# A new instruction order for a delta-rule attention and MLP kernel, with the clock-filler matmuls in other places

## Chip, core and metric

The kernel runs on one core of a Trainium2 chip. The metric is device time in microseconds for one execution of the whole program, all loads and stores included; lower is better.

## What is computed

Four batches of eight heads run a delta rule over 768 steps with head dimension 48. The result, reshaped to (4, 768, 384), goes through a layer norm without bias and a two-layer MLP with a residual. The reference, cut to its core:

```python
k_n = k / (norm(k, axis=-1) + 1e-6)
for t in range(S):                                   # S = 768
    y[:, :, t] = einsum('bhd,bhde->bhe', q[:, :, t], state)
    v_old = einsum('bhde,bhd->bhe', state, k_n[:, :, t])
    state = state + beta[:, :, t] * einsum('bhd,bhe->bhde', k_n[:, :, t], v[:, :, t] - v_old)
x = y.transpose(0, 2, 1, 3).reshape(4, 768, 384)
xn = (x - mean(x)) / sqrt(var(x) + 1e-6) * g_ln
out = x + maximum(xn @ w_ch1, 0) @ w_ch2             # 384 -> 1536 -> 384
```

The two weight matrices arrive as 64-bit floats; everything else is 32-bit.

## The kernel before

The sequence is cut into 12 chunks of 64 steps, and all 32 heads of a chunk are worked on at once.

**Per chunk, attention.** Keys and queries are loaded and turned (TensorE transposes, L555, or a DVE transpose, L577). The gram product of the keys is made in tiles of 48 rows by 32 columns (L606, later L674). From it comes the inverse of a small triangular matrix per head, by forward substitution on DVE: a long chain of short multiply and subtract instructions (L752/L759 for the first chunk, L843/L850 for pairs of later chunks). The query product (L637) is masked on DVE (L653). For chunk 0 only, two products (L806, with a copy on ACT, L809, between them) join the halves of the inverse, and DVE writes the result back (L813). Three small products (L902) with ACT copies (L908) and one DVE subtraction (L906) between them give the new values `u`; then come the output (L913), the state update (L923), and the reads of the state (L880).

**Per chunk, layer norm and MLP.** ACT copies the output out (L950). DVE and ACT make the statistics (L956 to L965) and the normalised rows (L968). They are transposed (L1000 on TensorE for the first three chunks, through DRAM later) and scaled into `xnt` (L1006, L1016). Chunks 0 to 2 use plain first-layer matmuls (L1178, 128x128 by 256 columns, six matmul records to a step); later chunks use a form with 15 products in place of 18 (L1094). The second layer is L1200 for chunk 0 and a form with seven products in place of eight (L1275) after it. These four lines use the whole 128x128 array.

**Weights.** Twelve pieces of 768 KB are loaded by ACT's DMA queue (L373), called p0 to p11 here. p0 to p5 are `w_ch1` (p0 to p2 hold the first half of its columns), p6 to p11 are `w_ch2`. Each is converted from 64 to 32 bits by two ACT instructions (L514, L522), one on DVE (L519) and one on GpSimd (L532). A staging buffer is free for its next piece when GpSimd has read it.

**Fillers.** Three steps of two 512-column matmuls on zeros (`fill`, L544) and 26 steps of two 256-column matmuls (`warm`, L1358) compute nothing that is used. They exist to keep TensorE's clock up while the first chunks are prepared. Once their constants exist, they wait for nothing but their place in TensorE's order.

**What sets the order.** The program builds a list of 2780 steps, and a tuple of step numbers, `ORDER`, says in which order they are emitted. Within one engine the emitted order is kept: each engine works through its own steps first in, first out, and an ACT or SyncE instruction that starts a load holds up those behind it until the load may start.

```python
    def emit(self, order):
        done = set()
        for n in order:
            s = self.steps[n]
            ...
            s.fn()
...
    def zeros():
        nc.tensor.matmul(f_[0][:, 256:512], ident, ident[:, 0:1].to_broadcast([128, 256]))
...
    with in_this_order(tc):
        line.emit(ORDER)
```

Of the kernel before, what the change touches and what calls it, by code (L numbers as in the profile page):

```python
# [57 lines left out]
def pool(n):  # L58
# [7 lines left out]
    18, 21, 5, 0, 6, 7, 78, 68, 20, 23, 9, 22, 24, 28, 125, 77, 70, 15, 8, 10, 12, 13, 30, 40, 27, 34, 31, 59, 16, 26, 29, 50, 33, 89, 39, 32, 35, 88,  # L66
    90, 60, 91, 92, 93, 25, 94, 126, 127, 61, 71, 1, 65, 47, 37, 38, 99, 128, 19, 129, 130, 131, 132, 133, 169, 135, 219, 2, 134, 136, 73, 100, 101,
    103, 102, 104, 36, 323, 137, 53, 321, 42, 138, 139, 140, 46, 63, 87, 76, 84, 56, 109, 107, 48, 322, 43, 352, 114, 105, 202, 115, 116, 106, 108,
    117, 118, 119, 120, 45, 51, 11, 74, 170, 324, 52, 58, 141, 142, 143, 4, 144, 145, 85, 146, 147, 148, 149, 150, 171, 151, 152, 44, 41, 96, 95, 121,
    98, 172, 153, 154, 155, 156, 157, 158, 159, 160, 161, 162, 163, 164, 165, 166, 167, 168, 174, 221, 124, 123, 57, 122, 3, 222, 55, 192, 97, 220,  # L70
    223, 173, 224, 17, 204, 225, 226, 228, 227, 230, 231, 232, 233, 234, 235, 236, 237, 238, 239, 240, 241, 175, 72, 83, 176, 177, 207, 14, 242, 243,
    208, 244, 245, 110, 111, 203, 54, 178, 246, 209, 113, 112, 179, 180, 200, 181, 86, 326, 293, 213, 206, 325, 182, 190, 194, 294, 211, 205, 183,
    247, 248, 229, 383, 249, 250, 251, 79, 252, 191, 703, 210, 328, 198, 217, 295, 296, 81, 297, 69, 298, 300, 362, 188, 253, 254, 255, 256, 257, 193,
    302, 299, 327, 301, 75, 258, 259, 357, 260, 305, 195, 199, 261, 215, 329, 336, 382, 303, 304, 306, 355, 310, 262, 263, 319, 311, 186, 307, 64,
    264, 265, 266, 267, 212, 268, 363, 333, 320, 269, 308, 184, 196, 330, 334, 842, 339, 82, 337, 840, 388, 341, 343, 387, 340, 66, 338, 342, 569,
    270, 312, 309, 317, 271, 272, 273, 187, 62, 313, 390, 201, 274, 389, 391, 49, 67, 189, 318, 275, 80, 185, 197, 392, 315, 214, 344, 331, 335, 316,
    314, 394, 276, 277, 278, 365, 353, 427, 367, 332, 358, 428, 425, 431, 393, 345, 279, 280, 426, 429, 281, 282, 283, 284, 285, 286, 287, 288, 289,
    290, 216, 350, 346, 432, 435, 218, 385, 564, 570, 430, 433, 349, 364, 291, 436, 354, 568, 292, 384, 705, 386, 395, 488, 439, 563, 368, 567, 566,
    565, 571, 434, 396, 707, 560, 715, 739, 561, 735, 437, 713, 487, 356, 366, 370, 489, 397, 360, 351, 398, 438, 464, 441, 399, 490, 491, 400, 440,
    492, 493, 359, 443, 401, 442, 404, 361, 372, 405, 407, 408, 411, 402, 562, 895, 494, 369, 495, 445, 371, 377, 406, 446, 465, 466, 449, 409, 403,  # L80
    450, 451, 452, 467, 497, 498, 410, 499, 500, 501, 502, 414, 415, 412, 503, 504, 505, 468, 572, 416, 506, 507, 413, 508, 573, 509, 444, 447, 373,
    453, 510, 374, 511, 574, 417, 512, 421, 704, 576, 454, 716, 513, 514, 422, 714, 515, 712, 717, 706, 701, 702, 734, 710, 708, 711, 718, 742, 746,
    748, 738, 743, 749, 375, 577, 376, 420, 423, 578, 419, 380, 424, 455, 448, 456, 516, 479, 378, 579, 418, 517, 518, 519, 580, 480, 469, 470, 457,
    458, 471, 520, 379, 381, 575, 581, 582, 521, 583, 709, 522, 841, 843, 839, 744, 1174, 733, 736, 747, 737, 745, 459, 606, 607, 523, 524, 525, 526,
    527, 528, 529, 530, 531, 460, 584, 461, 472, 473, 474, 475, 585, 719, 608, 612, 476, 724, 586, 587, 720, 481, 610, 532, 533, 482, 750, 723, 590,
    725, 613, 609, 614, 611, 616, 617, 615, 618, 721, 620, 722, 726, 619, 624, 534, 535, 536, 537, 588, 625, 589, 592, 591, 595, 538, 496, 485, 622,
    539, 483, 540, 541, 542, 543, 544, 545, 546, 547, 548, 549, 550, 484, 596, 597, 732, 621, 727, 728, 623, 639, 850, 640, 641, 642, 643, 626, 644,
    848, 628, 846, 851, 740, 993, 1209, 852, 1208, 478, 849, 730, 741, 729, 627, 731, 751, 752, 629, 847, 462, 838, 463, 994, 845, 1179, 630, 631,
    593, 594, 853, 1001, 1007, 477, 1004, 598, 551, 755, 602, 632, 633, 637, 636, 647, 646, 666, 667, 668, 669, 649, 650, 651, 1366, 645, 753, 756,
    893, 634, 890, 635, 638, 648, 600, 757, 605, 754, 656, 758, 759, 760, 604, 764, 761, 670, 763, 599, 601, 671, 657, 658, 652, 552, 553, 554, 555,  # L90
    556, 486, 557, 558, 672, 681, 762, 1173, 1172, 1207, 1000, 1005, 1175, 1003, 682, 683, 684, 653, 654, 685, 766, 655, 559, 854, 663, 659, 686, 674,
    660, 675, 676, 677, 678, 661, 1206, 1370, 1002, 997, 1006, 855, 856, 662, 891, 603, 767, 768, 769, 770, 771, 898, 899, 844, 999, 896, 858, 859,
    860, 857, 765, 772, 773, 775, 861, 892, 1008, 679, 687, 904, 900, 901, 680, 776, 862, 777, 778, 779, 863, 692, 693, 780, 781, 782, 783, 784, 1182,
    1177, 1187, 1181, 1367, 1185, 995, 998, 785, 906, 786, 689, 922, 664, 694, 695, 905, 925, 688, 864, 347, 787, 923, 788, 865, 789, 790, 791, 910,
    866, 1472, 1369, 1178, 1176, 1470, 792, 867, 793, 1183, 794, 1471, 795, 1009, 796, 1188, 869, 1364, 665, 673, 868, 870, 696, 697, 698, 902, 907,
    797, 911, 700, 872, 699, 1010, 916, 1184, 1363, 873, 798, 1186, 799, 1011, 917, 996, 800, 348, 903, 801, 877, 1205, 1012, 924, 1013, 897, 690,
    931, 871, 878, 1180, 874, 932, 933, 926, 934, 935, 875, 802, 1014, 803, 804, 912, 1015, 879, 805, 876, 806, 908, 807, 881, 808, 1016, 880, 909,
    913, 809, 882, 914, 928, 1017, 927, 810, 938, 918, 811, 915, 929, 1189, 936, 894, 919, 1018, 812, 884, 920, 939, 1019, 1628, 813, 885, 814, 958,
    886, 921, 959, 815, 937, 960, 930, 816, 1368, 961, 1022, 691, 940, 817, 1377, 1020, 818, 883, 819, 962, 1374, 820, 963, 821, 1204, 948, 822, 949,
    774, 1473, 823, 941, 964, 950, 824, 1469, 965, 951, 1021, 888, 952, 887, 1375, 955, 973, 825, 974, 1379, 1054, 953, 826, 1373, 942, 957, 827, 943,  # L100
    1631, 944, 1058, 1190, 954, 956, 1023, 1025, 945, 1210, 1194, 975, 976, 1026, 1191, 946, 1195, 1062, 1196, 947, 889, 828, 1029, 829, 1061, 1192,
    977, 830, 966, 1193, 1055, 1063, 967, 831, 968, 1056, 832, 978, 1059, 969, 833, 1057, 979, 970, 971, 1197, 972, 1030, 834, 1031, 1065, 835, 836,
    1202, 837, 1198, 1024, 1068, 1066, 1067, 1045, 984, 1069, 985, 1035, 986, 1199, 1203, 1027, 1070, 1047, 1200, 1028, 1201, 1032, 1212, 1071, 1060,
    1048, 1211, 987, 1064, 1213, 1072, 1049, 1033, 1034, 1074, 1052, 1036, 988, 989, 1073, 1037, 1081, 1376, 990, 1053, 1075, 1214, 1365, 1468, 1079,
    1050, 1215, 1632, 1076, 981, 1046, 1040, 1216, 1077, 1038, 1083, 1080, 1078, 1039, 1082, 1395, 1092, 1378, 1217, 1051, 1041, 1086, 1084, 1372,
    1095, 980, 1087, 1371, 1089, 1088, 1098, 1093, 1090, 1218, 1094, 1085, 1099, 1101, 1110, 1104, 1219, 1096, 1111, 1112, 1380, 1100, 1113, 1042,
    1114, 1105, 1115, 1091, 1102, 1120, 1641, 1116, 1220, 1103, 1044, 1636, 1107, 1097, 991, 1121, 1043, 1221, 1249, 983, 1222, 1108, 1925, 1246,
    1381, 1627, 1247, 1118, 1821, 1122, 1385, 1637, 1245, 1127, 1825, 1250, 1128, 1386, 1123, 1474, 1382, 1819, 1124, 1383, 1387, 1253, 982, 1384,
    992, 1117, 1125, 1388, 1823, 1106, 1630, 1109, 1129, 1393, 1119, 1126, 1137, 1389, 1390, 1138, 1139, 1248, 1391, 1140, 1252, 1396, 1141, 1251,
    1130, 1131, 1132, 1397, 1145, 1398, 1392, 1136, 1142, 1146, 1399, 1135, 1147, 1143, 1148, 1133, 1400, 1149, 1144, 1401, 1150, 1134, 1152, 1151,  # L110
    1153, 1403, 1224, 1402, 1154, 1163, 1254, 1256, 1223, 1404, 1227, 1255, 1394, 1155, 1405, 1225, 1258, 1156, 1406, 1164, 1228, 1407, 1232, 1157,
# [1362 lines left out]
```

## Time and profile before

| | |
|---|---|
| median of 3 runs | 510.86 us (510.31 to 513.01) |
| the profiled execution's own time | 511.47 us |
| its span, first to last instruction | 509.8 us |
| mean granted TensorE clock | 0.973 |
| busy | PE 96%, DVE 75%, POOL 48%, ACT 36% |
| matmuls | 9688 |

The profiled execution ran 0.61 us over the median, and 1.7 us of its time lies outside the span. In timeline rows the first number is the start in us from the span's start, the second the duration; what stands in square brackets is the engine's idle time before the row and what ended it. PEclk is the clock that was granted to TensorE as a share of full speed.

### The profile page before, as it was taken

How to read it: one execution, taken by the hardware profiler on the slowest of the kernel's cores; microseconds unless marked ns; L12 is line 12 of the kernel's file. 1: busy time of each engine (PE TensorE's matmuls, PEld its weight loads, DVE VectorE, ACT ScalarE, POOL GpSimd, SP SyncE). 2: the span in 40 equal slices, each digit the busy share in tenths (PEclk: the TensorE clock that was granted, in tenths of full speed). 3: DMA queues.
4: the chain of work that ended last, by engine and by line, in shares of the span. 5: the costliest groups of instructions: out<-in, count | busy, mean ns of one | idle time of the engine just before them, and what ended most of it. 6: DMA issues, size and time to landing. Idle time of an engine off the chain costs nothing.

```text
span 509.8 us, 21948 instructions
## 1 busy us (share of the span) xinstructions
PE 490.7 (96%) x9688; PEld 442.9 (87%) x9688; DVE 384.3 (75%) x854; ACT 185.4 (36%) x402; POOL 246.0 (48%) x377
## 2 busy tenths in 40 slices
PE   8669899999999999999999999999999999999996
PEld 5647787668898899999999989999999999999996
DVE  1886886989879997739999848999979889454241
ACT  3464864413532225162223434313431421424130
POOL 5122347111663267784191374391682581735544
PEclk9875899999999999999999999999999999999999
DMA  9984676454534550440363441530420302003011
GB/s 132 188 277 83 161 138 131 95 81 69 89 51 70 105 111 14 102 76 7 88 110 67 100 68 44 102 62 1 108 55 32 87 3 81 17 16 80 1 39 32
DMA packets 155855, 40.47 MB, mean 79 GB/s; under 512 B 149232, under 2 KB 152304, under 8 KB 155760
## 3 DMA queue, kind: packets, MB, share of 16 engines
q1 hardware_dynamic: 151760, 29.21, 31.8%
q10 hardware_dynamic: 3712, 9.83, 5.9%
q8 instruction: 76, 1.25, 1.0%
q14 instruction: 19, 0.16, 0.1%
q0 software_dynamic: 288, 0.03, 0.1%
HBM read 30.79 MB, written 8.26 MB: 77 GB/s over the span
## 4 chain that ended last, share of the span: by engine, by line
PE 89%; ACT 3%; DVE 2%; DMA 2%; issue 2%; SPq 1%; POOL 1%; ACTq 0%; DVEq 0%; POOLq 0%
PE f L1275 29%; PE f L1094 23%; PE f L1178 10%; PE two L902 6%; PE f L1200 3%; PE two L674 3%; PE by L913 2%; PE by L880 2%; PE two L880 2%; PE f L1358 2%; PE two L923 1%; DMA words<-in_moe_w_ch_dram 1%; PE two L637 1%; SPq L373 1%; ACT goff L627 1%
## 5 line engine op out<-in xcount | busy, mean ns | idle before, releaser
L1261 POOL TENSOR_TENSOR h_all<-h_all 128x256 f32<-128x256 f32 x99 | 75.5, 775 | 21.2 <-ACT h_all L1187 15.0
L1275 PE MATMUL f<-w_sb,h_all 128*128 128x192 f32 x396 | 81.6, 331 | 0.5 <-POOL xb L829 0.5
L850 DVE TENSOR_TENSOR xb<-xb,tmp 128x31 f32<-128x31 f32 (+15 forms) x186 | 75.8, 408 | 4.0
L1275 PE MATMUL f<-words,h_all 128*128 128x192 f32 x396 | 78.1, 331 | 0.7 <-DVE o L1293 0.7
L843 DVE TENSOR_TENSOR tmp<-xb,gb 128x31 f32<-128x31 f32 (+15 forms) x186 | 73.0, 392 | 4.3
L1107 DVE TENSOR_TENSOR h_all<-f,h_all 128x512 f32<-128x512 f32 x90 | 60.3, 683 | 20.0 <-PE f L1094 16.4
L1300 POOL TENSOR_TENSOR words<-h_all 128x128 f32<-128x128 f32 x66 | 30.3, 480 | 79.3 <-ACT h_all L1110 55.1
L1275 PEld LDWEIGHTS f<-words,h_all 128*128 128x128 f32 x396 | 65.1, 190 | 2.5 <-DVE o L1293 0.8
L1275 PEld LDWEIGHTS f<-w_sb,h_all 128*128 128x128 f32 x396 | 64.8, 190 | 2.2 <-POOL xb L829 0.8
L1178 PE MATMUL f<-xnt,w_sb 128*128 128x256 f32 x216 | 51.4, 386 | 0.5 <-DVE o L1293 0.5
L1102 ACT COPY h_all<-f 128x512 f32<-128x512 f32 x36 | 21.1, 586 | 72.7 <-PE f L1094 45.5
L1094 PE MATMUL f<-kt,w_sb 128*128 128x128 f32 x360 | 46.4, 277 | 0.0
L1110 ACT ACTIVATE h_all<-h_all 128x512 f32<-128x512 f32 x54 | 32.1, 625 | 38.5 <-DVE h_all L1107 38.4
L1178 PEld LDWEIGHTS f<-xnt,w_sb 128*128 128x128 f32 x216 | 39.7, 190 | 7.1 <-DVE o L1293 0.8
L1094 PEld LDWEIGHTS f<-kt,w_sb 128*128 128x128 f32 x360 | 43.4, 192 | 0.8 <-issue 0.4
L1094 PE MATMUL f<-xnt,w_sb 128*128 128x128 f32 x288 | 34.3, 276 | 0.0
L908 ACT COPY u<-two 128x768 f32<-128x768 f32 x24 | 19.1, 795 | 41.1 <-PE two L902 41.0
L1094 PEld LDWEIGHTS f<-xnt,w_sb 128*128 128x128 f32 x288 | 33.1, 192 | 0.1
L1293 DVE TENSOR_TENSOR o<-f,x 128x192 f32<-128x192 f32 x33 | 11.4, 348 | 22.7 <-PE f L1275 13.7
L1275 PE MATMUL f<-w_sb,words 128*128 128x192 f32 x132 | 28.2, 329 | 0.0
L532 POOL TENSOR_TENSOR w_sb<-words 128x768 uint32<-128x768 uint32 (+1 forms) x9 | 13.0, 1450 | 27.5 <-DVE words L519 15.2
L1293 POOL TENSOR_TENSOR o<-o,words 128x192 f32<-128x192 f32 x22 | 13.2, 608 | 26.9 <-DVE words L1293 23.4
(198 smaller groups left out, 883.2 us busy)
## 6 DMA issues: line engine op xcount, KB each, us to landing
words<-in_moe_w_ch_dram ACTq DMA_DIRECT2D x8, 768.0 KB, 5.7
v<-in_v_dram SPq DMA_DIRECT2D x24, 192.0 KB, 4.1
kr<-in_k_dram SPq DMA_DIRECT2D x46, 96.0 KB, 3.3
out_dram<-o SPq DMA_DIRECT2D x46, 96.0 KB, 2.4
xld<-xlt SPq DMA_DIRECT2D x9, 384.0 KB, 2.3
xnt<-xld SPq DMA_DIRECT2D x36, 96.0 KB, 2.8
tb<-in_q_dram SPq DMA_DIRECT2D x40, 64.0 KB, 2.6
tb<-in_k_dram SPq DMA_DIRECT2D x32, 64.0 KB, 3.2
```

The source lines that it names most:

```text
L843: lambda j=j, n=n, w=w, t=t: nc.vector.tensor_tensor(out=t, in0=xb[:, 0:n, j : j + 1].to_broadcast([128, n, w]), in1=gb[:, j : j + 1, j + ...
L850: "DVE", dve(n * w), lambda t=t, rest=rest: nc.vector.tensor_tensor(out=rest, in0=rest, in1=t, op=ALU.subtract),
L902: nc.tensor.matmul(*args(e, e ^ hp, 2 * j + hp))
L1094: nc.tensor.matmul(wide(p[:, 128 * n : 128 * n + 128]), w[:, 128 * n : 128 * n + 128], r, start=start and n == 0, stop=True, skip_group_ch ...
L1102: add("ACT", act(512), lambda: nc.scalar.copy(to[0], ps(p)), pk, to[1])
L1107: add("DVE", dve(512), lambda: nc.vector.tensor_tensor(out=to[0], in0=in0, in1=in1, op=op), [*pk, *y[1]], to[1])
L1110: add("ACT", act(512), lambda: nc.scalar.activation(to[0], to[0], ACTF.Relu), [], to[1])
L1178: nc.tensor.matmul(p[:, 0:TOK], w1_sb[:, t, f * 128 : (f + 1) * 128], xnt[:, t], start=(t == 0), stop=(t == KC - 1))
L1261: add(eng, cost, lambda: e.tensor_tensor(out=out_, in0=x, in1=y, op=op), r, w, port=2 if eng == "Pool" else 1)
L1275: lambda f=f, t=start and f == 0: nc.tensor.matmul(p[:, 0:D2], lhs(f), rhs[:, f], start=t, stop=(f == F2 - 1), skip_group_check=True),
L1293: lambda: e.tensor_tensor(out=out_, in0=a, in1=b_, op=ALU.add), r, w,
L1300: lambda f=f + i: e.tensor_tensor(out=s3[f], in0=one(0, 0)[0](f), in1=one(1, 0)[0](f), op=ALU.subtract),
```

## The change

Only `ORDER` differs: the same 2780 numbers in another sequence. The new sequence was made by a scheduler that takes the granted clock from the columns that matmuls stream, times the share of the array that they use, where the old one took it from the time that TensorE is busy. No step is added, removed or altered. Its first lines:

```diff
 ORDER = (
-    18, 21, 5, 0, 6, 7, 78, 68, 20, 23, 9, 22, 24, 28, 125, 77, 70, 15, 8, 10, 12, 13, 30, 40, 27, 34, 31, 59, 16, 26, 29, 50, 33, 89, 39, 32, 35, 88,
...
+    6, 7, 23, 5, 0, 59, 40, 60, 15, 8, 21, 4, 10, 20, 27, 16, 17, 219, 31, 26, 22, 69, 75, 29, 46, 35, 88, 89, 90, 67, 28, 25, 76, 92, 91, 93, 12, 94,
...
```

What that means for TensorE up to the first L1178 step (W = one `warm` step, F = one `fill` step; T0 to T3 = transposes of the keys of chunks 0 to 3, Tq0 and Tq1 of the queries, an a or b marks half of such a step pair; G = L606, Q = L637, J1 and J2 = the two L806 products, U1 to U3 = the three L902 products, Y = L913, S = L923, X = L1000, R = the first L880):

```
before: 4W F T0 F G0 F 2W T1a W T1b G1 4W T2 G2 2W J1 2W J2 Tq0 Q0 W T3a U1 T3b W U2 W U3 W
        Y W G3 S 2W Tq1 W X W X Q1 2W R L1178
after:  2F 2W T0 2W G0 3W F 3W T1 W G1 7W Tq0 T2 3W G2 Q0a W Q0b J1 J2 W U1 U2 T3a U3 W
        Y W T3b S W Tq1 X X G3 Q1 L1178
```

From U1 on there are ten W before the first L1178 step in the old order and three in the new one (one more W stands right ahead of U1 in the new order, and one ahead of T3a in the old one). The weight pieces are loaded in another sequence too:

```
before: p2 p6 p4 p3 p1 p0 p5 p8 p7 p9 p10 p11
after:  p2 p4 p0 p7 p6 p5 p1 p3 p9 p10 p8 p11
```

ACT's order around chunk 0's chain changes with it. In the new order a conversion of p0 (L522) stands directly ahead of the copy between J1 and J2 (L809), a conversion of p6 directly ahead of the copy after U1 (L908), and conversions of p4, p5 and p1 ahead of the copy after U3. On DVE two conversions of p2 (L519) move ahead of the transposes that make J1's operand (L774, L801), the mask of Q0 (L653) moves ahead of the first L843, and L813 follows 13 of the L843/L850 instructions where it followed 16. After the first L1178 step the same matmuls follow in a similar interleaving to the end. The very last GpSimd instructions change places: the sum that the last output needs (L1293) goes behind two others.

214 rows, old and new, of the table ORDER are left out of this document.

## The prediction

> **What bounds the kernel now.** I first read the page's totals and its slices.
>
> ```profile
> PE 490.7 (96%) x9688; PEld 442.9 (87%) x9688; DVE 384.3 (75%) x854; ACT 185.4 (36%) x402; POOL 246.0 (48%) x377
> ...
> PEclk9875899999999999999999999999999999999999
> ```
>
> TensorE (PE) is nearly always busy, and its clock is low only in the first five slices. The table of stretches splits the span there, at the start of Q1, the last product ahead of the MLP (columns: length, then busy us and count for PE, PEld, DVE, ACT, POOL, then clock, DMA share, GB/s).
>
> ```profile
> 0.00:61.30 61.30, 49.12 (x1262) 37.72 (x1262) 41.19 (x129) 34.03 (x63) 16.40 (x32) 0.78 0.75 173
> 61.30:506.00 444.70, 441.55 (x8429) 405.19 (x8428) 342.94 (x725) 151.38 (x339) 229.65 (x346) 1.00 0.34 66
> ```
>
> In the second row PE is idle for 3.2 of 444.7 us at full clock: no order of the same matmuls gains much there. The head is another matter: an eighth of the span, clock 0.78, 12 us idle. The same view in slices of the head shows what the clock follows:
>
> ```profile
> 17.70:21.10 3.40, 1.28 (x10) 0.94 (x8) 2.99 (x16) 0.58 (x2) 0.00 (x0) 1.00 0.99 312
> ...
> 41.60:45.00 3.40, 3.40 (x73) 2.62 (x71) 2.64 (x9) 1.40 (x2) 0.55 (x1) 0.50 0.00 0
> 45.00:48.40 3.40, 3.40 (x91) 2.27 (x94) 1.42 (x3) 1.90 (x4) 0.28 (x1) 0.50 0.29 37
> 48.40:51.80 3.40, 3.40 (x105) 2.63 (x98) 2.80 (x7) 1.35 (x3) 0.00 (x0) 0.50 0.60 113
> ```
>
> From 41.6 to 51.8 PE is busy all the time and has half its clock, so busy time isn't what is rewarded; that part of the change's idea holds. Half clock reigns from 21.1 to 27.9 and from 34.7 to 55.2, 27.3 us. What ends the head, though, is chunk 0's chain, read from the timelines of ACT, PE and DVE:
>
> ```profile
> 29.61 0.60 ACT L809 ACTIVATE xn<-f 128x512 f32<-128x512 f32 x1
> 32.85 0.91 ACT L514 ACTIVATE words<-words 128x768 f32<-128x768 f32 x1 [2.64 <-DMA words<-in_moe_w_ch_dram]
> 49.52 0.80 ACT L908 COPY u<-two 128x768 f32<-128x768 f32 x1 [2.63 <-PE two L902]
> ```
>
> ```profile
> 33.33 1.01 PE L806 MATMUL f<-xt,xn 32*32 32x32 f32 x96 [2.62 <-issue]
> ```
>
> ```profile
> 24.62 0.71 DVE L801 STREAM_TRANSPOSE xn<-xt 128x512 f32<-128x512 f32 x1
> ...
> 37.56 0.73 DVE L813 COPY_PREDICATED xt<-mask,f 128x512 f32<-128x512 int32 x1
> 40.18 1.22 DVE L653 TENSOR_TENSOR pt<-two,pmask 128x1024 f32<-128x1024 f32 x1 [1.33 <-PE two L637]
> ```
>
> L801 ends at 25.33; J1, L809 and J2 follow, J2 with 2.62 us of waiting on instruction issue (0.77 more falls on Q0); L813 ends at 38.29. Then Tq0, Q0, L653 (41.40) and T3a come ahead of U1 (41.98). U3's ACT copy ends at 50.32, L950 at 53.06, the normalised rows (L968) at 59.42, and the first L1178 starts at 64.74.
>
> **The change: chunk 0's chain.** I follow the new order with the old durations, each engine first in, first out.
> - *To L801.* Two L519 (0.36, 0.35) move in ahead of it and wait for p2's conversion, some 0.7 in all: end 26.1.
> - *J1.* Q0 now stands ahead of it and needs key and query copies that ACT makes after three conversions of p2 (0.55 each; p2 lands at about 21, as before). J1 runs at about 28 to 29.3, where it ended at 28.39.
> - *L809.* It stands behind a conversion of p0. That load starts with the gdiag copy (L623), at about 26.05. Such loads took 5.0 to 6.1 us from issue to use when nothing was queued before them (p2: 14.66 to 20.82), so p0 can be used at 31.2 to 32.2, and with 0.58 for the conversion L809 ends at about 32.7: 2.5 us **later**.
> - *J2, L813.* J2 needs 1.3 without the issue wait: 34.2. DVE is some 2 us into its next instructions then; L813 ends at about 37.0, 1.3 earlier.
> - *U1.* L653 has been done since about 30, and only one W separates L813 from U1: 37.2, where it was 41.98. This is the change's main gain, 4.8 us, and it comes from moving Q0, not from the clock.
> - *U1 to U3.* Half clock still holds by my count (few W left), so each takes 1.50 as before, against 0.88 for the same line in the dense stage. ACT's copies wait for loads: behind p0 are queued p7, p6, p5, p1. A piece is 786 KB, and the head moved 238 to 301 GB/s where loads were queued: 2.6 to 3.3 us each, taken as 3.0. So p6 can be used at about 38.2, p1 at about 44. With two conversions of p1 (0.56, 0.57) and the copy (0.80), U3's copy ends at about 46.1, where it was 50.32.
> - *Y to the MLP.* Y 2.1, the L950 copies to 48.9 (before 53.06); the layer norm on DVE behind fewer forward-substitution steps, to 54.1 (59.42); X, then Q1 behind ACT's copies, to 57.3; L1178 at 57.3.
>
> - *The queues.* On SyncE a load of chunk 1's values moves up (0.60 of issue), and Tq1's loads now stand behind one that waits for U3 (44.2): they land by about 50, Tq1 needs them at 52. On GpSimd the `g_ln` load (4.2 to land) is issued at about 49.5 behind three L532 and lands ahead of L1016 at 56. Both are covered; each us that U3 slips is passed on anyway.
>
> That is the shortest form of the chain. The old one, worked in the same way, lacks the two issue waits, 2.62 + 0.77 = 3.4 us. Between none and 3.4 of such waits I put 2.2, nearer the old sum since the same small matmuls run: first L1178 at 59.5, 5.2 us earlier.
>
> **Fillers.** A W in the late head takes 1.22 at half clock, 0.60 at full. Ten stand between U1 and the first L1178 before, three after. Most ran while PE waited for ACT or DVE; on the chain lay two ahead of J1 (1.1), one ahead of U2 (0.9) and part of one ahead of Y (0.2). The seven W that now follow G1 run while DVE is in its substitution and cost nothing; if DVE were done early they would cost 0.43 each. These sums are inside the times above.
>
> **The dense stage.** The matmuls are the same. What order changes is the step from small to full-array matmuls: six L1178 records take 1.29 us after full-array work and 1.49 after small, and the other full-array lines differ by the same 0.2. Both orders have 70 such steps behind the first L1178. Added up by line and predecessor, the new order has 0.8 us more, since R (1.08 and a switch) now comes behind the first L1178. Its waits before were these:
>
> ```profile
> PE two L923 <- ACT u L908: 0.9, 1, 0.9
> PE f L1275 <- DVE o L1293: 0.7, 1, 0.7
> PE f L1178 <- DVE o L1293: 0.5, 1, 0.5
> PE f L1275 <- POOL xb L829: 0.5, 1, 0.5
> ```
>
> The 0.9 arose because L923 of chunk 2 followed U3 at once; in the new order an L1178 step (1.49) stands between, which covers the ACT copy. The 0.5 at L1178 is opened likewise. For every step I compared the PE work between a matmul and the one that uses its result through other engines with those engines' durations: the tightest three are short by 0.03 us or less (before: 0.96 and 0.52). This counts no queueing, which made the other two waits (1.2), and a GpSimd conversion of `w_ch2` now comes late enough to cost L1200 up to 1.5 us near 84. I take 1.4 saved and 1.0 new.
>
> **The tail.** The last sum that the final output needs (L1293, POOL 0.59) moves behind two others; the final DVE sum, which started at 505.82, starts 0.25 later.
>
> **Sum.** -5.2 + 0.8 - 0.4 + 0.25 = -4.55 on the profiled execution's 511.47: 506.9. That execution ran 0.61 over the median of 510.86, so I expect 506.3 as a median.
>
> **A rule against it.** The Trainium skill ("TensorE: Matmul & The Clock Gate", part 1) says that the gate follows how busy PE has recently been, and that its 3.4 us windows run free of the kernel's start. The slices at 41.6 to 51.8 contradict the first half. By the second, fillers can't be aimed at a window, and the order's clock would vary from run to run; no run here shows it.
>
> **Rivals.**
> - *Loads decide (slower).* The new order puts L809 and both L908 copies right behind conversions that wait for a load. For: ACT already waited 2.64 for words, and the `w_sb` loads show 8.4 us to landing. Against: bandwidth is there once the small loads have ended. If the four pieces behind p0 take 5 us each, U3's copy comes 7.9 later: 514.2. It turns to a loss above 4.1 us a piece. 15%.
> - *Half clock runs into the MLP.* Between Y and L1178 few full-array columns stream (two W, no credit seen for transposes). The shortest stretch at half clock before was 6.8 us; if it lasts for 3.4 to 6.8 us of L1178, half of that, 1.7 to 3.4, is lost: 508.0 to 509.7. The skill's busy rule would give the same, as PE waits longer there. 14%.
> - *Nothing moves.* Another wait in the head replaces Q0's, or new waits in the dense stage eat the gain: 509 to 511. 7%.
> - *The clock does rise.* If fillers hold full clock from J1 to Y, the U products shrink by 0.62 each and Y by 0.95: 503.5. 8%.
>
> **How the numbers follow.** The forecast has 56%, with its own range 504.0 to 508.2 (issue waits of 0 to 3.4, dense waits of 0 to 2). A measurement of this kernel can tell about 0.5%, 2.6 us, from no change: faster means under 508.3. Forecast and rising clock make 0.64; half clock and nothing moves 0.20, with 0.01 of theirs beyond; loads deciding, with that 0.01, 0.16. The range of eight in ten leaves out most of the loads' case and half of the rising clock's: 503 to 512.5.
>
> **What would show it.** Right: L653 ends ahead of the first L843; U1 starts at 36 to 39; the first L1178 at 57 to 61; the stretch from there to the end as long as before within 2 us; half clock in 14 to 27 us of the head. Wrong: ACT idle for words ahead of L809 or L908 by more than 4 us in one place; L1178 at half clock; waits of over 3 us behind the first L1178.

## The result and the profile after

The new order takes 506.75 us (median of 4 runs, 505.78 to 508.88), the old one beside it 511.94 (4 runs, 510.31 to 513.58): a ratio of 0.991, 95% interval 0.988 to 0.9939 (the quotient of the two medians is 0.990). The profiled execution of the new order took 508.88 us, the longest of its four, with a span of 507.2. One execution each of the kernels e4 (518.28 us), e5 (807.76) and e8 (518.05) fell into a slower state of the chip: the ratios leave these out, and since those of e4 and e5 are the profiled ones, only the times of e4 and e5 are used.

The totals and the clock row of the page:

```profile
PE 489.8 (97%) x9688; PEld 443.1 (87%) x9688; DVE 384.5 (76%) x854; ACT 186.0 (37%) x402; POOL 246.1 (49%) x377
...
PEclk9955899999999999999999999999999999999999
```

The same stretches as before, with two of the slices of the head:

```profile
0.00:61.30 61.30, 51.00 (x1335) 40.33 (x1336) 43.64 (x134) 34.96 (x67) 17.93 (x33) 0.78 0.79 182
61.30:506.00 444.70, 438.75 (x8354) 402.79 (x8353) 340.84 (x721) 151.09 (x336) 228.21 (x344) 1.00 0.34 66
...
45.00:48.40 3.40, 3.18 (x70) 2.41 (x70) 3.37 (x9) 1.60 (x3) 0.03 (x1) 0.50 0.74 223
48.40:51.80 3.40, 3.40 (x69) 2.63 (x68) 3.30 (x9) 2.13 (x5) 2.07 (x3) 0.50 0.86 176
```

In the first 61.3 us PE now gets through 1335 matmuls instead of 1262, at the same mean clock of 0.78. Half clock reigns in one piece from 27.2 to 54.5 instead of two; it adds up to 27.3 us, as before. The other runs say the same: the mean granted clock was 0.975 in the 94 runs of the old order that stand beside the experiments (0.966 to 0.986 from run to run), 0.975 in the four of the new one. So the clock, which the new scheduler was about, gave nothing. The chain of chunk 0, from the timelines of ACT, PE and DVE (start, duration, and in brackets the idle time before the row):

```profile
29.91 0.56 ACT L522 ACTIVATE h_all<-h_all 128x384 uint32<-128x384 uint32 x1 [2.51 <-DMA h_all<-in_moe_w_ch_dram]
35.84 0.60 ACT L809 ACTIVATE xn<-f 128x512 f32<-128x512 f32 x1 [5.37 <-DMA w_sb<-in_moe_w_ch_dram]
...
47.81 0.80 ACT L908 COPY u<-two 128x768 f32<-128x768 f32 x1 [1.31 <-PE two L902]
```

```profile
27.80 0.91 PE L637 MATMUL two<-kq 48*64 48x64 f32 x20 [3.33 <-issue]
...
34.82 0.96 PE L806 MATMUL f<-xn,kt 32*32 32x32 f32 x54 [2.70 <-issue]
...
38.27 0.96 PE L806 MATMUL f<-xt,xn 32*32 32x32 f32 x54 [0.51 <-issue]
...
40.32 1.50 PE L902 MATMUL two<-v,xt 32*32 32x48 f32 x64
...
59.73 2.86 PE L1178 MATMUL f<-xnt,w_sb 128*128 128x256 f32 x12
```

```profile
24.26 0.71 DVE L801 STREAM_TRANSPOSE xn<-xt 128x512 f32<-128x512 f32 x1
...
30.98 1.23 DVE L653 TENSOR_TENSOR pt<-two,pmask 128x1024 f32<-128x1024 f32 x1 [4.26 <-PE two L637]
...
39.29 0.74 DVE L813 COPY_PREDICATED xt<-mask,f 128x512 f32<-128x512 int32 x1 [0.49 <-PE f L806]
```

The last two of PE's rows were these in the old order:

```profile
41.98 1.50 PE L902 MATMUL two<-v,xt 32*32 32x48 f32 x64
...
64.74 1.56 PE L1178 MATMUL f<-xnt,w_sb 128*128 128x256 f32 x6
```

L653 is out of the way at 32.21 (before: 41.40), yet U1 starts only 1.7 us earlier (40.32, before 41.98). The reason stands in PE's brackets: Q0 waited 3.33 us on instruction issue and J1 2.70. The 5.37 of L809 is put down to a load of `w_sb`, which L809 doesn't read: J1 ended at 35.78, and L809 followed at once. The first L1178 starts at 59.73, where it was 64.74; 1.08 of these 5.0 us is R, which has moved behind it. Behind it, PE's waits are these (total, times, longest):

```profile
PE f L1094 <- DVE knrms L835: 1.1, 1, 1.1
PE two L674 <- DVE s_all L932: 0.8, 1, 0.8
PE f L1178 <- issue: 0.6, 1, 0.6
PE f L1275 <- POOL h_all L1261: 0.2, 1, 0.2
```

All four old waits (2.64) are gone and 2.96 of new ones are there. From the first L1178 to the last sum on DVE it is 443.57 us, before 441.08: 2.5 more, of which 1.08 is R. The rest need not be the order's doing: e3 and e6 below have the same steps behind that L1178 and take 441.8 and 441.3.

### The profile page after: what moved, and what is told of

It reads as the page before. It is cut to its first block, busy times and chain, and to the rows that moved or that the text cites. A ratio compares the mean times of both kernels' runs of the same rounds, so it can differ in the third digit from the quotient of the medians.

```text
span 507.2 us, 21959 instructions
## 1 busy us (share of the span) xinstructions
PE 489.8 (97%) x9688; PEld 443.1 (87%) x9688; DVE 384.5 (76%) x854; ACT 186.0 (37%) x402; POOL 246.1 (49%) x377
## 4 chain that ended last, share of the span: by engine, by line
PE 73%; DMA 6%; POOL 6%; SPq 6%; DVE 4%; issue 3%; ACT 1%; POOLq 0%; DVEq 0%; ACTq 0%
PE f L1275 21%; PE f L1094 20%; PE f L1178 7%; SPq L373 6%; PE two L902 5%; POOL h_all L1261 3%; PE f L1200 3%; PE f L1358 3%; PE two L674 2%; PE two L880 2%; PE by L880 2%; DMA xnt<-xld 2%; PE by L913 1%; PE two L923 1%; POOL kt L1077 1%
## 5 line engine op out<-in xcount | busy, mean ns | idle before, releaser
L843 DVE TENSOR_TENSOR tmp<-xb,gb 128x31 f32<-128x31 f32 (+15 forms) x186 | 75.5, 406 | 4.5
L1275 PE MATMUL f<-words,h_all 128*128 128x192 f32 x396 | 76.2, 330 | 0.3 <-POOL h_all L1261 0.2
L850 DVE TENSOR_TENSOR xb<-xb,tmp 128x31 f32<-128x31 f32 (+15 forms) x186 | 72.7, 391 | 3.8
L1178 PE MATMUL f<-xnt,w_sb 128*128 128x256 f32 x216 | 51.5, 385 | 0.6 <-issue 0.6
L1094 PE MATMUL f<-kt,w_sb 128*128 128x128 f32 x360 | 46.3, 276 | 1.1 <-DVE knrms L835 1.1
L1178 PEld LDWEIGHTS f<-xnt,w_sb 128*128 128x128 f32 x216 | 39.9, 190 | 7.0 <-issue 1.2
L1094 PEld LDWEIGHTS f<-kt,w_sb 128*128 128x128 f32 x360 | 43.3, 192 | 1.8 <-POOL kt L1077 1.3
L908 ACT COPY u<-two 128x768 f32<-128x768 f32 x24 | 19.1, 798 | 57.3 <-PE two L902 41.9
L1293 POOL TENSOR_TENSOR o<-o,words 128x192 f32<-128x192 f32 x22 | 13.2, 609 | 51.8 <-DVE words L1293 51.8
L1094 PE MATMUL f<-xnt,w_sb 128*128 128x128 f32 x288 | 34.7, 277 | 0.0
L1094 PEld LDWEIGHTS f<-xnt,w_sb 128*128 128x128 f32 x288 | 33.4, 192 | 0.2
L1293 DVE TENSOR_TENSOR o<-f,x 128x192 f32<-128x192 f32 x33 | 11.3, 346 | 22.8 <-PE f L1275 16.9
L1187 ACT ACTIVATE h_all<-f 128x256 f32<-128x256 f32 x36 | 13.2, 384 | 38.0 <-PE f L1178 37.4
```

The source lines that it names most:

```text
L843: lambda j=j, n=n, w=w, t=t: nc.vector.tensor_tensor(out=t, in0=xb[:, 0:n, j : j + 1].to_broadcast([128, n, w]), in1=gb[:, j : j + 1, j + ...
L850: "DVE", dve(n * w), lambda t=t, rest=rest: nc.vector.tensor_tensor(out=rest, in0=rest, in1=t, op=ALU.subtract),
L1094: nc.tensor.matmul(wide(p[:, 128 * n : 128 * n + 128]), w[:, 128 * n : 128 * n + 128], r, start=start and n == 0, stop=True, skip_group_ch ...
L1178: nc.tensor.matmul(p[:, 0:TOK], w1_sb[:, t, f * 128 : (f + 1) * 128], xnt[:, t], start=(t == 0), stop=(t == KC - 1))
L1275: lambda f=f, t=start and f == 0: nc.tensor.matmul(p[:, 0:D2], lhs(f), rhs[:, f], start=t, stop=(f == F2 - 1), skip_group_check=True),
L1293: lambda: e.tensor_tensor(out=out_, in0=a, in1=b_, op=ALU.add), r, w,
```

## Experiments

Each kernel differs from the new or the old one in `ORDER` unless said otherwise. Ratios are to the old order, measured on the same chip in the same session.

| kernel | median us | ratio, 95% interval | first L1178 in its profile |
|---|---|---|---|
| new order | 506.75 | 0.991, 0.988 to 0.9939 | 59.73 |
| e1 new head | 515.44 | 1.01, 1.0068 to 1.0131 | 59.99 |
| e2 old head | 518.18 | 1.0151, 1.0105 to 1.0196 | 64.63 |
| e3 old fillers | 507.99 | 0.9948, 0.9928 to 0.9968 | 61.05 |
| e4 Q0 ahead | 512.02 | 1.0024, 1.0005 to 1.0044 | not used |
| e5 Q0 late | 509.36 | 0.9975, 0.9957 to 0.9994 | not used |
| e6 no late W | 506.62 | 0.9929, 0.9899 to 0.9959 | 56.72 |
| e7 new to 175 us | 505.65 | 0.9907, 0.9886 to 0.9928 | 58.83 |
| e8 old to 175 us | 511.45 | 1.0006, 0.9988 to 1.0024 | 66.46 |
| e9 small loads | 507.09 | 0.9941, 0.992 to 0.9963 | 57.11 |
| e10 w_ch2 later | 508.65 | 0.9979, 0.9952 to 1.0006 | 61.32 |
| e11 the same, no late W | 509.29 | 0.9981, 0.9955 to 1.0007 | 59.85 |
| e12 six W | 511.69 | 1.0028, 1.0005 to 1.0051 | 61.60 |

**Where the gain lies: e1, e2, then e7, e8.** My theory was the chain ahead of the first L1178; the rival was the order of the dense stage.

```diff
-    line.emit(ORDER)
+    line.emit(head + [n for n in other if n not in head])   # e1: new head, e2: old head
```

> The new order up to the first L1178, the old order for all that is left. Chain theory (the gain is chunk 0's chain ahead of the first L1178, 64.74 before and 59.73 after): first L1178 at about 60.8, since R (1.08) now comes ahead of it again, the rest 441 us long as before; 3.9 us gained, ratio about 0.992. Dense-stage theory (the order behind the first L1178 brings the gain): ratio 0.998 to 1.002.

> The old order up to the first L1178, the new order for all that is left. Chain theory: first L1178 at about 64.7, the rest some 1.3 us longer than before (the new waits of 2.96 for the old ones of 2.64, one switch more), ratio about 1.002. Dense-stage theory: ratio about 0.991, the whole gain.

Both came out slower than either whole order, so neither theory can be read from the times. The waits of e1's PE behind the first L1178 show why:

```profile
PE f L1178 <- ACT h_all L1187: 7.3, 1, 7.3
PE two L923 <- ACT u L908: 0.9, 1, 0.9
PE f L1178 <- DVE o L1293: 0.5, 1, 0.5
PE f L1275 <- POOL xb L829: 0.5, 1, 0.5
```

One wait of 7.3 at 70 us: an ACT copy (L1187) stands behind a conversion that waits for a weight piece (ACT is idle 5.62 us for it). The two orders fetch the last pieces in different sequence and the joint cuts through that, which is the likely reason. e2 has the same wait with 3.4. The other three rows are the old order's own. The head itself behaved as I expected: L1178 at 59.99 with R (1.08) ahead of it. The pair was repeated with the joint behind the last weight load:

> The first 951 steps of the new order, then the rest in the old order. The joint lies behind the last weight load, where the two orders differ in 15 steps only (174 us into the new profile, 180 into the old one). Chain theory: the 5.9 us gained up to there stay, and the rest takes 325.9 as before, where the new order takes 329.3: ratio 0.985 to 0.990. Dense-stage theory: ratio 0.998 to 1.002.

> The first 956 steps of the old order, then the rest in the new order. Chain theory: nothing gained ahead of the joint, 2 to 3.4 us lost behind it: ratio 1.003 to 1.007. Dense-stage theory: ratio 0.989 to 0.993.

e7 has the whole gain, if a little less than expected, and e8 has none. Everything the change brings is made in the first 175 us; how much of it ahead of the first L1178 this pair doesn't tell. The 2.5 us that the profile shows as lost behind the first L1178 do not show in the times: e7 and the new order have the same ratio, and e8 equals the old order.

**Q0: e4 and e5.** The prediction put the main gain down to Q0 standing ahead of J1.

```diff
-old: ... G2 2W J1 2W J2 Tq0 Q0 W T3a U1      # L653 behind L813
+e4:  ... G2 2W Tq0 Q0 J1 2W J2 W T3a U1      # L653 ahead of J1's users
-new: ... G2 Q0a W Q0b J1 J2 W U1             # L653 ahead of the first L843
+e5:  ... G2 W J1 J2 Q0a Q0b W U1             # L653 behind L813
```

> The old order with one move: Tq0, its two copies, Q0 and the mask product L653 stand ahead of J1. Chain theory: 3.7 us (L813's end 38.29 to U1's start 41.98) shrink to the 1.0 of T3a, and J1 starts later by Q0's 1.1 to 2.2; U1 starts 1 to 3 us earlier than 41.98: ratio 0.994 to 0.998. Filler theory: ratio 0.999 to 1.003, since fillers stand where they stood.

> The new order with one move back: Q0 stands behind J2 again and the mask product L653 behind L813, all else as in the new order. Prediction's step (moving Q0 makes the main gain): Q0 (1.1 to 2.2 at half clock) and L653 (1.22) come back between L813 and U1, U1 starts 3 to 4 us later than 40.3 and the ratio to before rises from 0.991 to 0.996 to 0.999. Rival (waits for instructions set the time to U1, whatever stands there): J1 comes free of Q0's wait of 3.33 and starts near 26 instead of 30.85, L813 ends 3 to 5 us earlier, U1 starts at 38 to 41 and the ratio stays at 0.988 to 0.993.

Putting Q0 back (e5) raises the ratio from 0.991 to 0.9975: of the gain of 9 in a thousand some 6 hang on Q0's place (the two intervals leave 2 to 11). That is what the prediction's step said. But moving Q0 alone in the old order (e4) gains nothing, against my expectation (the filler theory's number came true), so the place alone is not enough. The new order also has Tq0 and its copies ahead of T2 and G2, and other places on ACT and DVE; which of these it takes stays open, since e4's profile is not used. One thing the expectation left out can be worked out from the old profile, though no run shows it: the work that stands on ACT ahead of Q0's two copies in e4 ends at 29.59 there. So Q0 could start only some 4 us behind 26.48, where J1 started before, and J1 comes behind Q0; the expectation had J1 only 1.1 to 2.2 later.

**Fillers: e3 and e6.**

```diff
-new: ... Q0a W Q0b J1 J2 W U1 U2 T3a U3 W Y W T3b S W Tq1 X X G3 Q1 L1178
+e3:  ... Q0 W J1 2W J2 U1 U2 W T3a U3 W Y W T3b W S 2W Tq1a W Tq1b X W X G3 Q1 2W L1178
+e6:  ... Q0a Q0b J1 J2 U1 U2 T3a U3 Y T3b S Tq1 X X G3 Q1 L1178
```

> The new order with each of the 29 fillers behind that PE step behind which it stood in the old order (two ahead of J1 and two behind it, seven between U1 and Q1). Chain theory: the fillers cost at most the two ahead of J1, 1.2 to 2.4 us, the rest is hidden: ratio 0.991 to 0.996. Filler theory (their places make the gain, by clock or by PE time): ratio 0.998 to 1.002 and the half clock back in two stretches.

> The new order without its last five fillers that stand behind G2 and ahead of the last one (of those between Q0's halves, ahead of U1, behind U3, behind Y and behind S0). If a filler costs what it takes where PE doesn't wait (1.22 at half clock): those between Q0's halves and ahead of U1 lie on the chain, 2.4 us, the one behind U3 some 0.2; first L1178 2.0 to 2.6 us earlier, ratio 0.986 to 0.989. Granted-clock theory (full-array columns hold the clock up): the slices from 47.7 to 54.5 carry two fillers and without them the clock stays at half one or two stretches of 3.4 us longer, into Q1 and L1178, which costs 1.2 to 3.4 us back: ratio 0.990 to 0.995.

With the old places of the fillers 5 in a thousand of the 9 stay, and L1178 starts 1.3 us later, as the chain theory has it; the half clock is back in two stretches, as the filler theory had it, but adds up to less (23.9 us). So the new places may be worth up to 4 in a thousand, with two intervals that leave anything from nothing to 9. Without five late fillers the profile has L1178 at 56.72, but it is that of the fastest of 8 runs (503.52), and their median doesn't move (0.9929 against 0.991, intervals overlap). The chain theory's 0.986 to 0.989 missed; the granted-clock rival's 0.990 to 0.995 was met. In the profile half clock ended earlier (25.3 to 49.2), against that rival; over the 8 runs, though, the mean clock was 0.971 where the new order's four have 0.975, so the rival isn't refuted.

**The waits on issue: e9, e10, e11.** Counted from the start, each of PE's long waits on issue in the head stands in front of the 477th matmul (Q0 or J1), the 605th (J1 or J2) or the 733rd (J2 or Q0), and each later one at or a few records short of a place some multiple of 128 further on (861st, 989th, 1117th, 1373rd). The exceptions are waits in front of U1, of 0.39 to 2.14 us in six profiles (e3, e6, e8 to e11), which the profile also calls issue; there U1 starts 0.1 us behind the end of L813 (in e8 of L653). The page names a queue that fits:

```profile
q8 instruction: 76, 1.25, 1.0%
```

76 packets of 16 KB each; PE has 2 x 9688 = 19376 matmuls and weight loads, 255 to a packet. So a packet holds about 128 matmuls with their weight loads, and PE waits where the next one isn't there. The times of the packets in the trace's DMA records bear this out. In the new order three of them land at 26.29, 33.37 and 36.86, and Q0, J1 and J2 go on at 27.80, 34.82 and 38.27. In all twelve profiles (those of the table without e4 and e5, and the old order's) the 51 waits of over 0.2 us at such places in the first 90 us end 1.2 to 1.8 us behind the landing of a packet. J1 and J2 are 128 matmuls each; J2 took 1.46 us of PE at full clock in the old order (0.45 and 1.01), so such a packet is used up quickly. Does the traffic of the weight loads set how long PE waits for the packet? e9 changes the amount loaded and no place of any step (four GpSimd instructions that clear the buffers come in as well):

```diff
     def fetch(i, **kw):
...
+        if i in (1, 5, 6, 7):
+            dst, src = dst[..., 0:128], src[..., 0:128]
         dma("ACT", dst, src, 256, 115, w=WORD_KEYS[BUF[i]], **kw)
```

> The new order, with four weight loads made small: of p7, p6, p5 and p1, issued at 26.8, 29.9, 35.9 and 36.3 in the new profile, only 0.39 of 3.15 MB is fetched (GpSimd clears their buffers ahead of that, where it was idle; the rest of those weights is left out of the computation). Every instruction of TensorE stays where it was. Theory 'loads stretch the instruction fetch': the waits on issue at TensorE's 605th and 733rd matmul (2.70 and 0.51 in the new profile; 0.8 to 2.2 and 1.6 to 3.5 in three other kernels that share this head) fall below 0.7 in sum, while the one at the 477th, at 24 to 28 us with p0 and p4 in flight, stays above 1; U1 starts at 35 to 38 and the ratio to before is 0.975 to 0.987. Rival 'a block of instructions takes 4 to 5 us whatever else is loaded': the three waits still sum to 4 us or more, U1 starts at 38 to 41 and the ratio stays at 0.988 to 0.994.

PE's rows of e9 (its lines are numbered 4 higher: L810 is J1 and J2, L906 is U1):

```profile
25.99 0.91 PE L641 MATMUL two<-kq 48*64 48x64 f32 x20 [2.12 <-issue]
...
30.82 0.96 PE L810 MATMUL f<-xn,kt 32*32 32x32 f32 x54 [0.51 <-issue]
...
34.27 0.96 PE L810 MATMUL f<-xt,xn 32*32 32x32 f32 x54 [0.51 <-issue]
...
38.52 1.50 PE L906 MATMUL two<-v,xt 32*32 32x48 f32 x64 [2.14 <-issue]
```

The waits in J1 and J2 sum to 1.02, against 2.4 to 4.4 in the six profiles with the same head and full loads (new order, e1, e3, e6, e7, e12); the one at the 477th, with p0 and p4 still loading, stays at 2.12. That is more than the 0.7 that I expected, but below all six. The packets show where the time goes: each takes 0.9 to 1.6 us with full loads and with few, but from PE going on at one edge to the start of the next packet it was 3.95 and 1.12 us in the new order (the packets for J1 and J2), 1.93 and 1.10 in e9. The two add up to 4.3 to 6.0 us in the six, to 3.0 in e9, and to 3.7 and 2.4 in e10 and e11 below, which have fewer loads there. So the loads do stretch the fetch, mostly ahead of the packet; each kernel has one profile. But my number for the time was wrong: the ratio is 0.9941, no better than the new order. The last row tells why: J2 ended at 35.23, yet U1 waited until 38.52. That wait isn't at a packet's edge (it is the 789th matmul); it follows L813, and DVE's timeline of e9 shows L813 behind the forward substitution in DVE's own order:

```profile
29.18 1.23 DVE L657 TENSOR_TENSOR pt<-two,pmask 128x1024 f32<-128x1024 f32 x1 [3.06 <-PE two L641]
...
37.46 0.33 DVE L847 TENSOR_TENSOR tmp<-xb,gb 128x175 f32<-128x175 f32 x1
37.71 0.71 DVE L817 COPY_PREDICATED xt<-mask,f 128x512 f32<-128x512 int32 x1
```

(L817 is L813, L657 is L653.) It has no idle time before it: DVE was busy with 13 steps of the substitution that stand ahead. With the waits on issue in J1 and J2 cut, DVE's order is the next bound, and only 1.8 us of U1's start are won. These 1.8 us are just what L653 starts earlier by (29.18, in the new order 30.98): L653 waits for Q0, and so for the packet at the 477th matmul, and DVE needs 7.7 to 9.0 us from there until it is ready for L813 in every profile with this head. In the new order it was ready at 38.80, and J2's end held L813 up for only 0.49 more. Nor are the 1.8 us clear of the spread: with full loads U1 started at 37.24 to 39.10 in e1, e3, e6 and e7. Then I tried to use it in a kernel that computes everything, from e7:

```diff
-e7:  ACT: ... p7 ... p6 ... L809 ... [L522 of p6] L908 p3 ...
+e10: ACT: ... L809 ... L908 p7 p3 p6 ... L1016 [L522 of p6] ...
```

> The kernel of new order up to 175 us and old order behind it (0.9907), with the loads p7 and p6 (weights that the second MLP product needs at about 78 us) issued behind U1's copy, at about 41, where they stood at 26.7 and 29.3; p6's conversion (L522) goes behind the normalised rows' copies (57 us). Theory 'loads stretch the instruction fetch': of the waits on issue between L801 and U1 (2.04, 0.23 and 3.52 in that kernel's profile) one to three us go, U1 starts at 36 to 38 instead of 39.1; ratio 0.983 to 0.988. Rival 'the fetch takes as long anyway', or the loads that are left fill the gap: ratio 0.989 to 0.993. If the two loads come back as waits of the second product near 80 us: above 0.993.

> The same, and without the last five fillers behind G2. Chain theory: with shorter waits on issue the fillers between Q0's halves and ahead of U1 lie on the chain, 1 to 2.4 us: ratio 0.980 to 0.986. Granted-clock theory: the clock comes back one stretch of 3.4 us later and this costs 1 to 2 us: ratio no lower than that of the kernel with the fillers.

U1 starts at 37.23 in e10, as expected, and the times are still worse than e7's. PE's rows, and the stretches of 4 us from 44 on (1.6 MB of weights move in the first of them, 0.2 in the second and none in the third, where the many small packets of another queue keep the DMA engines busy, as in e7):

```profile
30.79 0.96 PE L806 MATMUL f<-xn,kt 32*32 32x32 f32 x54 [0.96 <-issue]
...
34.24 0.96 PE L806 MATMUL f<-xt,xn 32*32 32x32 f32 x54 [0.51 <-issue]
...
46.52 1.09 PE L913 MATMUL two<-u,pt 64*64 64x48 f32 x29 [0.71 <-issue]
...
53.82 0.45 PE L923 MATMUL two<-u,kr 64*64 64x48 f32 x5 [1.47 <-issue]
```

```profile
44.00:48.00 4.00, 3.29 (x79) 2.36 (x75) 3.57 (x9) 1.84 (x4) 1.58 (x2) 0.50 1.02 405
48.00:52.00 4.00, 4.00 (x83) 3.29 (x76) 3.54 (x12) 3.31 (x8) 1.87 (x3) 0.50 1.02 148
52.00:56.00 4.00, 2.53 (x22) 1.81 (x15) 2.24 (x7) 1.68 (x3) 0.00 (x0) 0.50 0.73 118
```

The waits came back at later packets (Y and S), with the DMA engines busy for 0.73 of the time or more, and half clock lasted until 60.1 instead of 52.7 as in e7: Q1 and what stands ahead of it ran at half speed. L1178 started 2.5 us later than in e7. Waits of the second product near 80 us, the third possibility, don't show in the profile, which is that of the fastest of e10's 12 runs. e11 has the ratio of e10, so its two theories can't be told apart by the time; both had counted on a gain that wasn't there. The longer half clock fits a clock that follows columns, which the next paragraph counts.

**The clock: e12.** In each run the clock changes on a grid of 3.413 us. For eleven profiles (all of those above without e4, e5 and e12) I added up, for each cell of that grid from 3 to 89 us, the time that its matmuls' columns take at full clock, times the share of the array that each uses (the figure that the kernel's program has for each step). With 1.3 us or more in a cell the next cell had full clock in 171 of 171 cases (11 of them from half clock); with under 0.8, in none of 55; between, in 10 of 44. The marks were chosen on these same cells, and one cell or the other crosses them when a matmul across an edge is shared out in another way (counted so, a cell of e3 with 1.32 was followed by half clock). PE's busy time doesn't separate them: of 15 cells at half clock with PE busy throughout and under 1.3 us of such columns, 10 were followed by half clock. The old order has an example of both: its cells from 41.6, 45.0 and 48.4 hold 1.1, 0.8 and 1.0 us of columns and stay at half clock, the next holds 1.4 and full clock follows, and PE is busy throughout in all four. (The counts in the text below have e4 with them.)

```diff
-new: ... J1 J2 W U1 U2 ...
+e12: ... J1 J2 6W U1 U2 ...
```

> The new order with six fillers in a row ahead of U1 where it has one: 4.4 us more on TensorE at half clock (five at 0.87), of which some 0.8 hide behind L813. Rule 'the clock of the next stretch of 3.4 us follows the columns streamed in this one, times the share of the array' (in eleven profiles 172 of 172 stretches at full clock and 13 of 13 at half clock with at least 1.3 us of such columns were followed by full clock, and none of 59 with under 0.8): the six carry 2.6 us of columns in at most 5.7 us, the clock comes back ahead of U1 or inside it, U1 takes about 0.9 instead of 1.50, later fillers and products gain up to 1.7, and the time grows by 1 to 3 us over the new order: ratio to before 0.993 to 0.997. Rule 'busy time': TensorE was busy there before; U1 keeps 1.50 and the ratio is 0.997 to 1.001.

PE's rows of e12 (lines 1 higher: L1359 is W, L903 the U products):

```profile
39.04 5.38 PE L1359 MATMUL f<-ident 128*128 128x256 f32 x12
44.35 0.89 PE L903 MATMUL two<-v,xt 32*32 32x48 f32 x64
46.15 0.88 PE L903 MATMUL two<-u,goff 32*32 32x48 f32 x64 [0.91 <-ACT u L909]
...
48.17 1.50 PE L903 MATMUL two<-v,xt 32*32 32x48 f32 x64 [0.55 <-DVE v L907]
```

The clock came back at 44.2 and U1 and U2 take 0.89 and 0.88 instead of 1.50; with few columns in their cell it falls again at 47.6, and U3 has 1.50. That is as the rule of columns has it: 1.8 us of them in the cell from 40.8, 0.9 in the next. It isn't a test against busy time, as I had meant it to be: in the new order PE is busy for 2.02 of the same cell's 3.41 us, and with six W for all of it, so a rule of busy time would bring the clock back too. What speaks against busy time is the count above, and in e12 the cell from 74.9: PE is idle for 0.55 us of it at half clock, it holds 1.4 us of columns, and full clock follows. The extra W don't pay: they cost more than the two products win, and L1178 starts 1.9 us later. The time is worse than I expected by some 3 us: the profile has a wait of 2.96 on issue in an L1178 at 75.5, at a packet's edge again (0.56 there in the new order), and one more stretch of half clock with it (74.9 to 78.3).

## Why the prediction was right, and where it was not

- *The total.* 506.3 was predicted, 506.75 measured; faster, as the forecast had it. A gain of 4.55 us was worked out, the ratio makes it 4.6. The head's -5.2 came as -5.0 in the pair of profiles, and e7 and e8 show that the whole gain lies in the first 175 us. That the median came within 0.5 us is in part luck: the four runs lie 3.1 us apart, and the old order's median moved from 510.86 to 511.94.
- *To L801* (26.1): it ended at 24.97. p2's words were there in time, and the two L519 cost nothing.
- *J1, L809, J2.* L809 was to end at 32.7 behind the load of p0; it ended at 36.44. The load cost what I took (5.8 from issue to use), but the waits on issue were mis-sized: 2.2 in the sum, 7.0 measured between Q0 and U2. I had taken the old kernel's 3.4 as the upper end. Only part of it reached the end of the chain: Q0's 3.33 lies beside the load of p0, and J1's and J2's 3.21 lie, but for 0.49, beside the 7.8 us that DVE needs from L653 to L813. The working had this path by DVE (L813 at 37.0, J2 at 34.2), but not that it starts at Q0: a wait in front of Q0 shifts all of it, waits in J1 and J2 only what is longer than it. Against the sum without such waits (57.3) the chain came 2.4 late, which is the 2.2 that I put there: the right amount by two errors that cancel.
- *U1* (37.2 without waits, "36 to 39"): 40.32, a little outside; the same head, with some fillers elsewhere or left out in two of them, started U1 at 37.2 to 39.1 in the profiles of e1, e3, e6 and e7. That the main gain needs Q0's place is shown by e5; that this place makes it alone is not what e4 shows. And 4.8 us was too much in this profile: 1.7 there.
- *U1 to the MLP.* 20.1 predicted (37.2 to 57.3), 19.41 measured, 22.76 before; 1.08 of the difference is R, which has moved behind L1178. Without R the head wins 3.9, and more of it behind U1 (2.3) than up to it (1.7). The loads of the rival "loads decide" never held ACT for more than 2.51 us at a stretch.
- *The half clock.* 27.3 us, just above "14 to 27"; it did not reach L1178. Both other clock rivals failed in this kernel; in e10 half clock comes near L1178 (60.1, with L1178 at 61.3).
- *Dense stage and tail.* I took 1.4 saved, 1.0 new and 0.8 for the switches and R: 0.4 more. The profile has 2.4 more: 2.64 saved, 2.96 new, R 1.08 and about 1 spread over the lines. In e3 and e6, with the same steps there, it is 0.7 and 0.2 more than in the old order's profile, so that much of the 2.4 is spread from run to run. The new waits at L674 and L1094 are for DVE instructions; the comparison that should have found them counted no queueing. The wait of up to 1.5 at L1200 did not come. The last sum starts 0.24 behind the last matmul, before 0.11: a loss of 0.13, where I took 0.25.
- *The rule against it.* The Trainium skill ("TensorE: Matmul & The Clock Gate", part 1) lets the gate follow how busy PE has been, in windows that run free of the kernel's start. The second half is now seen: the grid begins 0.59 us into the span in the old order's profile, 3.29 in the new one's, 1.36 in e2's. The prediction added that an order's clock would then vary from run to run: over 94 runs of the old order it went from 0.966 to 0.986. The first half is not what these runs show, as above.

## What to carry to other kernels

When an order is changed, follow the chain that ends the slow stage step by step, and ask at each step which engine's queue is next if the wait goes: here cutting two waits (e9) only uncovered DVE's order. Bursts of small matmuls next to heavy loads pay in waits on issue that no dependency shows; find them by counting matmuls. To join two orders, cut where they have done the same set of steps, above all the same loads, or the joint costs more than what is tested.

## What the runs showed that I had not expected

- PE's waits on issue stand 128 matmuls apart, at the edges of 16 KB packets of instructions; with few loads in flight they were 0.51 us in J1 and J2 (e9), the longest was 4.5 (e2's J2). The packet lands 1.2 to 1.8 us before PE goes on and takes 0.9 to 1.6 us itself; what varies most is when it starts, and what delays that can't be told from these runs, but for the part of the loads in e9.
- The clock of the next 3.413 us follows the columns streamed in this one, times the share of the array: full in all but at most a few of some 170 cells with 1.3 us of them, in none of 55 with under 0.8. This is a count over the runs of one kernel; no run here changes the columns and leaves PE's busy time alone.
